# A recurrent attention layer with a Fourier mixer on one core: 64-token steps in quarters of the array, and mixing products of two chunks summed in PSUM

## The chip, the cores and the metric

One core of a Trainium2 chip runs the whole kernel. The metric is the device time of one execution in microseconds (us); the median of three runs of the kernel before is 349.94 us.

## What is computed

The first half is an mLSTM layer, with 4 batch entries, 8 heads, 768 tokens and a head width of 40. For every head a 40x40 state and a normalizer are carried from token to token:

```python
m_new = np.maximum(f_gate[:, :, t] + m, i_gate[:, :, t])
f_stab = np.exp(f_gate[:, :, t] + m - m_new)
i_stab = np.exp(i_gate[:, :, t] - m_new)
C = f_stab * C + i_stab * outer(vt, kt)
n = f_stab * n + i_stab * kt
y[:, :, t] = sigmoid(o_gate) * (C @ qt) / np.maximum(np.abs(n . qt), 1.0)
```

The second half takes x, the heads side by side (4 x 768 x 320), and mixes tokens and channels:

```python
theta = x @ w_theta
zr, zi = x * np.cos(theta), x * np.sin(theta)
u = x + einsum('ts,bsd->btd', w_tok_r, zr) + einsum('ts,bsd->btd', w_tok_i, zi)
out = u + np.maximum(u @ w_ch, 0.0)
```

The four weight matrices arrive in float64 and are handed over as pairs of 32-bit words.

## The kernel before, in words

The 768 tokens are cut into 6 chunks of 128. A unit n is one chunk of one batch entry (24 units, `attention(n)`, L403); a mixer step q is one chunk of a pair of batch entries (12 steps, `mixer(q)`, L534).

**Attention, in chunked form.** A unit makes a 128x128 matrix of decay factors per head in a tile E of 8 x 128 columns. In the first chunk they come out of matmuls (`assemble`, L292) and one exponential per half (L421). In the five others a DMA spreads a row of gate sums over all partitions (L425, from DRAM scratch g_d) and ScalarE takes eight exponentials with a bias per token (L430). GpSimd then zeroes what lies above the diagonal (L436). The scores (`score`, L440) are eight float32 matmuls that contract 64 rows, four in each half of the array's rows. VectorE multiplies scores and factors (L449). The output (`pv`, L457) adds, in one PSUM bank, three matmuls of the scaled queries (`qs`, L453; their factors eb are also spread by a DMA) with the carried state C (L461), and eight full-array matmuls of weights with values (L464; L469 in the first chunk). VectorE makes the denominator (L474, L475), the gate (L480) and x (L486). The state is carried over a chunk by `fade` (L500 or L498), three matmuls (L506), `wane` (L516, L154, L156) and `grow` (L527).

A float32 matmul shows in the trace as two passes, each a weight load (PEld) and a matmul (PE); a float32r matmul shows as one. So the counts of the float32 lines are twice the matmuls of the code.

**Mixer.** x is turned (L542), split in a high and a low part in float32r (L544, L545), added to the accumulator acc (L550), multiplied by w_theta (L557, L563), reduced to a turn (L569, L573), put through sine and cosine (L582, L583), multiplied by x (L588) and split again (L589, L590). Then each of five column groups j takes 12 matmuls of 384 columns (`group`, L596, the line L601) into a two-bank PSUM tile, and VectorE adds that tile to acc (L616). For the first chunk two copies and one shorter add stand in its place (L608, L611, L612). That is 60 groups, each with an add of its own.

**Weights.** `split` (L330) rebuilds float32 from the float64 words on VectorE and ScalarE in seven steps (L338 or L340, L343, L344, L347, L350, L358, L359); two pieces per chunk, three and more elsewhere.

**The end** (`channel`, L620). Once all chunks are mixed, u is split (L656, L657) and multiplied by w_ch (L671, L681), VectorE adds the result (L691), and DMAs store it.

**PSUM.** Three slots of two banks (`two`) serve scores, first-chunk factors, x transposes, theta and mixing; two slots of one bank (`one`) serve the attention output and the state update.

**Order.** Every step is a task with a letter for its engine (T TensorE, V VectorE, A ScalarE, G GpSimd, D a DMA issued by SyncE). A list written out in the code, `ORDER`, gives number and engine of every task; each engine does its own tasks in that order, and waits are added where a tile is shared.

Of the kernel before, what the change touches and what calls it, by code (L numbers as in the profile page):

```python
# [8 lines left out]
F32 = mybir.dt.float32  # L9
# [13 lines left out]
KD = 3 * D  # L23
TOK = 9 * D + H * E1
# [4 lines left out]
HEAD = [3 * g + j for j in range(3) for g in range(3) if 3 * g + j < H]  # L29
RANK = [HEAD.index(h) for h in range(H)]  # L30
SPREAD = (0,)
# [4 lines left out]
LEAST = 2.0**-15  # L36
WCOLS = 1792

ORDER = """
4V 24T 0D 1D 2V 60V 62V 63V 3A 108D 67A 70D 61G 64V 68V 69G 65A 109V 82D 66V 71A 74D 83A 141D 124D 143T 145A 126T 111V  # L40
144A 84V 112V 148T 113V 72D 110G 131T 142D 125D 127A 114V 128A 75A 209T 147G 85V 116V 115D 129G 86V 73A 119T 208D 130G
132V 87A 146G 133V 150V 149V 76V 121V 88A 134T 77V 120A 151T 210A 78V 291D 89G 211A 192T 93A 135V 122A 152V 190D 79A
155G 136V 207D 153V 138G 101D 194A 213G 80A 193A 123D 293D 212G 214T 197T 195G 137V 102A 216V 154V 156T 157A 94D 158T
117T 196G 294D 139T 81G 215V 191D 199V 159A 118A 198V 217T 160V 295D 140V 95A 90A 161A 274D 103V 200T 92A 91A 218V
272D 162T 301G 297A 163T 104V 96V 105V 221G 296A 219V 276D 201V 202V 106A 275D 164A 204G 292D 220V 298G 360D 203V 165V
306G 299T 280T 300V 222T 356D 224T 278A 337D 277A 166V 273D 59G 282G 279G 362A 225V 223V 361A 226V 97V 167A 281V 302T
98V 227A 583D 168A 169V 402D 205T 228T 229T 364T 172V 341D 270D 170V 107G 357D 345T 303V 358D 99A 206A 230A 173A 171V
174V 271A 363G 231V 232V 283T 100G 365V 284V 285V 308G 187T 188V 304V 409D 233A 305V 289G 359D 234A 422D 418D 403A
287A 189V 178T 286V 235G 180V 410V 416D 307T 437D 343A 179V 184T 411V 366G 340D 186V 185V 238G 342A 412V 236A 309V
175T 367T 424A 239V 177V 338D 373A 344G 339D 176V 413V 346V 263D 368V 288T 414A 420D 310T 181T 311A 290V 369V 182V  # L50
312V 371G 347G 370V 441D 404V 419D 237V 348T 372T 352V 405V 183A 314T 423A 315T 354A 421D 442A 240G 313V 440D 406V
445T 439D 426T 374V 425G 415G 443A 316A 264A 317V 353T 444G 427V 244T 250T 355V 318A 446V 417A 428V 407A 433G 319A
349V 265V 320A 429T 253T 587D 350V 438D 351V 266V 267V 252A 268A 408G 246V 256D 324G 257A 245V 434T 255V 487D 435G
447G 436V 325A 483D 486D 430V 241T 488A 431V 251V 555D 448T 258V 489A 502D 259V 485D 321G 260V 247T 506D 254V 449V
452G 484D 242V 491T 450V 504D 248V 432V 322A 261A 454G 243A 510T 249V 490G 375T 451V 503D 507A 492V 376A 453T 505D
493G 508A 498V 262G 509G 455V 589A 648D 494T 377V 379T 326V 500G 499T 568D 588A 694D 495V 517G 511V 456T 380T 378V
381A 501V 269V 457A 496V 591T 512G 585D 323G 562D 382V 590G 383V 513T 564D 385A 458V 566D 556V 584D 695V 389G 331T
459V 384A 592V 386G 519V 586D 332V 569A 570A 565D 514V 563A 598G 515V 460T 652D 461T 516V 462A 572T 463V 327T 593G
328V 594T 390V 653A 497V 521T 567D 518T 571G 573V 574V 654A 391G 629D 464V 335T 524V 595V 466A 729D 522A 523V 333T
520V 596V 465A 387A 336V 525T 633D 388V 655G 467G 334V 656T 635A 634A 637T 600V 468V 526T 470G 597V 527A 557V 471V  # L60
528V 632D 657V 579A 472V 650D 575T 599T 576V 708D 649D 577V 529A 636G 394T 578V 601V 581G 638V 396T 397V 400T 530A
531A 651D 696V 658V 630D 602T 535G 631D 469G 580T 710D 395V 659T 603A 582V 709A 532V 639V 329T 401V 794D 640T 660V
558V 714D 604V 605V 398T 712D 330V 665A 663V 646V 715A 779D 732D 533V 781A 716A 536V 717G 731D 606T 733D 644G 661V
713D 559V 718T 399V 641V 642V 737T 711D 735A 607T 643V 662V 720G 534G 664T 719V 666V 721T 645T 734A 608A 697V 777D
730D 537G 698V 548D 739V 392T 795D 609V 736G 560A 561G 722V 546T 647V 780A 610A 854D 738V 667T 612A 727A 668A 547V
740T 393V 477T 611A 725A 549V 782G 798D 669V 538T 613V 741V 723V 670V 478V 540T 550V 797D 799A 775D 744G 616G 539V
671T 724V 551V 796D 860D 672T 701D 742V 746V 783T 778D 673A 541V 699V 785G 743V 913D 674V 802T 552V 542T 784V 871D
804G 800A 745T 553A 862A 801G 614A 803V 809A 617V 544T 618V 805T 700G 479T 675A 677A 747V 776D 681G 543V 847D 748T
811G 726T 856D 545V 475T 728V 749V 476V 676A 554G 750V 786T 480V 861A 932D 873D 678V 874D 481T 881G 682A 875D 787V
752T 751V 753T 702A 788V 789V 792G 858D 859D 482V 879T 848A 615G 806V 754A 864T 810T 755V 877A 876A 849V 807V 863G  # L70
865V 808V 683G 872D 878G 621T 756A 866V 880V 679V 619T 703V 813T 812V 758A 790G 814A 857D 620V 622V 680G 882T 931D
# [747 lines left out]
```

## Time and profile before

| | |
|---|---|
| runs | 349.94 us median, 349.14 to 351.73, three runs |
| span of the profiled execution, first to last instruction | 347.3 us |
| median of the runs less that span | 2.6 us |
| TensorE matmuls busy | 309.7 us (89% of the span), 2246 passes |
| VectorE (DVE) busy | 297.2 us (86%) |
| ScalarE (ACT) busy | 187.0 us (54%) |
| GpSimd (POOL) busy | 162.3 us (47%) |
| moved by DMA | 59.66 MB |

The page gives the profiled execution's time as its span; the 2.6 us are taken as what lies around it. A row of a group of instructions has, after the count, the time in which at least one of them ran, the mean length of one in ns, and then the idle time of the engine just before them with what ended it. Matmuls and weight loads overlap their neighbours, so for them the first figure divided by the count is the pace, and the mean length is not. PEld is the row of weight loads. [...]

### The profile page before, as it was taken

What the parts mean: (1) busy time and instruction counts of PE and PEld (TensorE: products, weight loads), DVE (VectorE), ACT (ScalarE), POOL (GpSimd) and SP (SyncE); (2) the same over time, 40 slices, a digit from 0 to 9 for tenths busy, and PEclk for the clock granted to TensorE, in tenths of its full rate; (3) what the DMA queues carried; (4) which work ended last, traced back from release to release, by engine and by line L of the source; (5) the groups of instructions that cost most, each with busy time, mean ns of one, the idle gap of its engine ahead of it and who ended that gap; (6) DMA issues with size and microseconds to landing.
All of it is one profiled execution on the core that took longest, in us unless ns stands there. A gap on an engine that the chain in (4) does not pass through costs nothing.

```text
span 347.3 us, 5976 instructions
## 1 busy us (share of the span) xinstructions
PE 309.7 (89%) x2246; PEld 295.6 (85%) x2246; DVE 297.2 (86%) x468; ACT 187.0 (54%) x375; POOL 162.3 (47%) x122
## 2 busy tenths in 40 slices
PE   1559886997999989898979999889999999999994
PEld 0559876987998979798979999889999999998994
DVE  2999999899999998999999969998999796897231
ACT  2857888937767688757539384649334221140000
POOL 0836675645486864531492258552128432644000
PEclk9969998799899989998999999999999999999999
DMA  4968999718469895096557775355301000001423
GB/s 145 346 215 285 327 366 318 271 32 295 162 205 303 262 295 196 9 286 215 165 178 278 259 262 156 98 144 174 116 3 45 2 0 0 2 0 47 161 113 136
DMA packets 20912, 59.66 MB, mean 172 GB/s; under 512 B 2191, under 2 KB 7700, under 8 KB 20884
## 3 DMA queue, kind: packets, MB, share of 16 engines
q1 hardware_dynamic: 20884, 59.28, 51.3%
q8 instruction: 18, 0.29, 0.3%
q14 instruction: 10, 0.08, 0.1%
HBM read 55.17 MB, written 4.10 MB: 171 GB/s over the span
## 4 chain that ended last, share of the span: by engine, by line
PE 54%; DVE 36%; DMA 4%; issue 3%; POOL 1%; ACT 0%; SPq 0%; DVEq 0%; POOLq 0%; ACTq 0%
PE two L601 28%; PE two L671 7%; PE one L464 5%; PE two L557 3%; DVE E L449 3%; PE two L445 3%; DVE val L347 3%; PE one L461 2%; DVE val L343 2%; DVE sg L480 2%; DMA w<-in_gates 2%; DVE val L344 2%; DVE z L590 2%; DVE C L527 2%; DMA tok<-in_tok 2%
## 5 line engine op out<-in xcount | busy, mean ns | idle before, releaser
L601 PE MATMUL two<-w,z 128*128 128x384 f32 x720 | 139.7, 350 | 8.2 <-DVE r L573 5.3
L601 PEld LDWEIGHTS two<-w,z 128*128 128x128 f32 x720 | 129.6, 196 | 10.9 <-DVE r L573 6.3
L616 DVE TENSOR_TENSOR acc<-two,acc 128x768 f32<-128x768 f32 x50 | 46.7, 949 | 8.7 <-PE two L601 8.5
L430 ACT ACTIVATE E<-E,biasT 128x128 f32<-128x128 f32 x160 | 49.4, 391 | 7.3 <-DMA E<-g_d 7.1
L436 POOL TENSOR_SCALAR_AFFINE_SELECT E<-E 128x1024 f32<-128x1024 f32 (+1 forms) x28 | 33.7, 1211 | 33.5 <-ACT E L430 30.9
L464 PE MATMUL one<-tok,E 128*128 128x41 f32 x320 | 42.7, 272 | 0.5 <-issue 0.4
L464 PEld LDWEIGHTS one<-tok,E 128*128 128x128 f32 x320 | 41.0, 193 | 0.9 <-DVE E L449 0.9
L449 DVE TENSOR_TENSOR E<-two,E 128x1024 f32<-128x1024 f32 (+1 forms) x28 | 29.4, 1060 | 2.0 <-POOL E L436 2.0
L461 PE MATMUL one<-C,q 120*128 120x123 f32 (+1 forms) x120 | 26.3, 301 | 2.9 <-DVE C L527 1.3
L671 PE MATMUL two<-u,w 128*128 128x384 f32 x156 | 28.5, 339 | 0.3 <-DVE acc L616 0.3
L445 PE MATMUL two<-qk 64*128 64x128 f32 x384 | 26.0, 285 | 2.8 <-DVE acc L550 1.5
L445 PEld LDWEIGHTS two<-qk 64*128 64x128 f32 x384 | 24.4, 196 | 4.6 <-DVE acc L616 1.8
L671 PEld LDWEIGHTS two<-u,w 128*128 128x128 f32 x156 | 26.8, 188 | 1.6 <-issue 1.0
L588 POOL TENSOR_TENSOR ab<-ab,X 128x640 f32<-128x640 f32 x10 | 16.3, 1631 | 19.5 <-ACT ab L583 19.5
L359 POOL TENSOR_TENSOR w<-val,w 128x768 fp32r<-128x768 f32 x9 | 18.4, 2043 | 13.8 <-ACT w L358 8.6
L691 DVE SCALAR_TENSOR_TENSOR acc<-two,acc 128x768 f32<-128x768 f32 x10 | 9.3, 954 | 17.2 <-PE two L681 9.3
L557 PE MATMUL two<-wth,xs 128*128 128x320 f32 x144 | 23.5, 312 | 0.5 <-DVE acc L550 0.5
L453 POOL TENSOR_TENSOR q<-q,eb 120x384 f32<-120x384 f32 x12 | 14.6, 1219 | 16.6 <-PE two L445 11.4
L557 PEld LDWEIGHTS two<-wth,xs 128*128 128x128 f32 x144 | 21.5, 188 | 0.9 <-issue 0.9
L461 PEld LDWEIGHTS one<-C,q 120*128 120x128 f32 x120 | 18.9, 192 | 4.0 <-issue 2.5
L590 POOL TENSOR_TENSOR z<-r,z 128x640 fp32r<-128x640 f32 x9 | 16.0, 1778 | 10.4 <-ACT z L589 5.3
L569 ACT ACTIVATE r<-two 128x640 f32<-128x640 f32 x11 | 7.7, 701 | 23.8 <-PE two L563 23.5
(120 smaller groups left out, 540.3 us busy)
## 6 DMA issues: line engine op xcount, KB each, us to landing
qk<-in_qk SPq DMA_DIRECT2D x24, 512.0 KB, 5.7
E<-g_d SPq DMA_DIRECT2D x20, 512.0 KB, 4.6
raw<-in_wtok SPq DMA_DIRECT2D x12, 768.0 KB, 7.0
tok<-in_tok SPq DMA_DIRECT2D x24, 344.0 KB, 6.5
out<-acc SPq DMA_DIRECT2D x10, 384.0 KB, 2.5
q<-in_q SPq DMA_DIRECT2D x20, 180.0 KB, 4.6
eb<-e_d SPq DMA_DIRECT2D x20, 180.0 KB
sg<-in_og SPq DMA_DIRECT2D x5, 640.0 KB, 7.7
```

The lines of the kernel that those rows point to most:

```text
L359: add(name + "_lo", "GV", lambda e: ENG[e].tensor_sub(lo(), v(), hi().bitcast(F32)), [val, *rest], step)
L430: nc.scalar.activation(u.E.t[:, r], u.E.t[:, r], AF.Exp, bias=biasT[:, c, b * H + r:b * H + r + 1])
L436: nc.gpsimd.affine_select(d, d, pattern=[[0, k], [1, P]], compare_op=ALU.is_ge, fill=0.0, base=0, channel_multiplier=-1)
L445: nc.tensor.matmul(u.sc.t[:, f, hp], u.qk.t[rows, 1, hp], u.qk.t[rows, 0, hp], start=True, stop=True)
L449: add(f"wg{n}{a}", "V", lambda e, a=a, z=z: nc.vector.tensor_mul(u.E.t.rearrange("p (f k) t -> p f (k t)", f=2)[:, a:z], u.sc.t[:, a:z], u ...
L461: nc.tensor.matmul(u.ph.t[:, 3 * g * E1:h1 * E1], u.q3.t[:KD, g, :], C[b][:, 3 * g:h1, :].rearrange("p h e -> p (h e)"), start=True, stop= ...
L464: nc.tensor.matmul(u.ph.t[:, h * E1:(h + 1) * E1], u.E.t[:, RANK[h], :], u.tok.t[:, 9 * D + h * E1:9 * D + (h + 1) * E1], start=False, sto ...
L557: nc.tensor.matmul(th.t[:, b, :DM], xs.t[:, x, k], wt5[:, y, k], start=(i == l == 0), stop=False)
L590: add(f"zl{q}{s}", "GV", lambda e, s=s, src=src: ENG[e].tensor_sub(zv(1, s), src.t, zv(0, s).bitcast(F32)), [src, z], n + 1.5)
L601: nc.tensor.matmul(pm.t[:, t, :TH], z.t[:, x, s, j * P:(j + 1) * P], wv(c, y, s, t), start=(k == 0), stop=(k == 5))
L616: add(f"ga{q}{j}", "V", lambda e, j=j, pm=pm, av=av: nc.vector.tensor_add(av, pm.t[:, :, :TH], av), [pm], n + 2.6 + 0.3 * j, swap="acc")
L671: nc.tensor.matmul(pm[jj].t[:, t, :TH], wcv(x)[:, col:col + P], up[pr, k][:, y, ts], start=(i == l == 0), stop=(jj == 2 and i == 4 and l = ...
```

## The change

Attention works in steps of 64 tokens: a unit is still 128 tokens of one batch entry, but it holds two steps. Its decay factors are 8 x 64 columns instead of 8 x 128, one step in one half of the partitions. All four products of a unit (scores, state update, carried state times query, weights times values) are 64-row, 64-column float32 matmuls that address the four quarters of the array in turn. The decay factors come from four float32r matmuls in every chunk, with the mask inside, so the DMAs that spread gate rows, the eight exponentials per unit and GpSimd's select are gone, and with them q3, eb, g_d and e_d. The state is kept in two copies per batch entry and carried twice per unit. The carried part leaves PSUM scaled by `pa` and is added by `hv`.

PSUM becomes four slots of two banks, for everything.

The mixing products of two consecutive chunks are added up in one PSUM tile before VectorE adds it to acc; `GROUPS` says which chunks go together, for each pair of batch entries.

`split` loses its clamp (a scaled absolute value on ScalarE takes its place) and its absolute value is always on ScalarE. Some steps may run on other engines, sigmoid works in halves, and `ORDER` is new.

The core of the diff, without the new order, the gate preparation (`gate_part`, which writes every gate sequence twice, shifted by 64 tokens) and the data layout:

```diff
+L = P // 2
+GROUPS = [[(0,), (1, 2), (3, 4), (5,)], [(0, 1), (2, 3), (4,), (5,)]]
...
-    two = slots("two", 3, [2, 512], pool=ps)
-    one = slots("one", 2, [512], pool=ps)
+    two = slots("two", 4, [2, 512], pool=ps)
...
-    E_k = slots("E", 3, [H, P], pool=ap)
+    E_k = slots("E", 3, [2, 4 * L], pool=ap)
...
-            nc.vector.tensor_scalar_max(v(), v(), LEAST)
-            nc.vector.tensor_scalar(vi(), vi(), 3, 0x3FFFFFF8, op0=ALU.logical_shift_left, op1=ALU.bitwise_and)
+        add(name + "_abs", "A", lambda e: nc.scalar.activation(v(), words(1).bitcast(F32), AF.Abs, scale=LESS), [rawt, val], step)
+        add(name + "_up", "V", lambda e: nc.vector.tensor_scalar(vi(), vi(), 3, None, op0=ALU.logical_shift_left), [val], step)
...
     def attention(n):
+        u.dd, u.sc, u.it, u.ph = Tile(two), Tile(two), Tile(two), Tile(two)
+        def assemble(e):
+            o = lambda f: u.dd.t[:, f, :4 * L].rearrange("p (k t) -> p k t", t=L)
+            for f in range(2):
+                nc.tensor.matmul(o(f), W(c)[:, f], M[:, b], start=True, stop=False)
+            for f in range(2):
+                nc.tensor.matmul(o(f), place[:, 2 * b + f], Gm(c), start=False, stop=True)
+        add(f"exp{n}", "A", lambda e: nc.scalar.activation(u.E.t, u.dd.t[:, :, :4 * L], AF.Exp), [u.dd, u.E], n - 0.5, table="exp")
+        def score(e):
+            for k in range(4):
+                for f in range(2):
+                    for x in range(2):
+                        s = slice(L * x, L * x + L)
+                        nc.tensor.matmul(u.sc.t[half[x ^ f], f, k * L:(k + 1) * L], q4(1)[half[f], k, s],
+                                         q4(0)[half[f], k, s], start=True, stop=True)
+        add(f"wg{n}", "V", lambda e: nc.vector.tensor_mul(u.E.t, u.sc.t[:, :, :4 * L], u.E.t), [u.sc, u.E], n)
+        def state(e):
+            for k in range(4):
+                for f in range(2):
+                    for x in range(2):
+                        r = half[x ^ f]
+                        h = 4 * f + k
+                        nc.tensor.matmul(u.st.t[half[f], x, k * E1:(k + 1) * E1], u.tok.t[r, h * D:h * D + L],
+                                         vt()[r, h], start=True, stop=True)
+        def carry(x):
+            add(f"cw{x}{n}", "GV", lambda e: ENG[e].tensor_mul(C[b][1 - x], C[b][x], f), (), n + 0.2)
+            add(f"up{x}{n}", "V", lambda e: nc.vector.tensor_add(C[b][1 - x], sv(x), C[b][1 - x]), [u.st], n + 0.3)
+        def inter(e):
+...
+                        nc.tensor.matmul(u.it.t[half[x], f, k * E1:(k + 1) * E1], q4(0)[half[f], k, s], C[b][x][half[f], k],
+                                         start=True, stop=True)
+        def intra(e):
+...
+                        nc.tensor.matmul(u.ph.t[half[x], f, k * E1:(k + 1) * E1], u.E.t[r, f, k * L:(k + 1) * L],
+                                         vt()[r, 4 * f + k], start=True, stop=True)
+        add(f"pa{n}", "VA", passed, [u.it, u.hv], n + 0.4)
+        add(f"hv{n}", "V", lambda e: nc.vector.tensor_add(hv4(), v4(u.ph), hv4()), [u.ph, u.hv], n + 0.5)
...
     def mixer(q):
+        mine = next(g for g in GROUPS[pr] if c in g)
+        if c != mine[-1]:
+            return
-                            nc.tensor.matmul(pm.t[:, t, :TH], z.t[:, x, s, j * P:(j + 1) * P], wv(c, y, s, t),
-                                             start=(k == 0), stop=(k == 5))
+                            nc.tensor.matmul(pm.t[:, t, :TH], Z[cc, pr].t[:, x, s, j * P:(j + 1) * P], wv(cc, y, s, t),
+                                             start=(k == 0 and cc == mine[0]), stop=(k == 5 and cc == mine[-1]))
+            for cc in mine:
+                add(f"mix{cc * 2 + pr}{j}", "T", lambda e, cc=cc, group=group: group(e, cc), [Z[cc, pr], w[cc], pm], n + 2.5 + 0.3 * j)
```

Read from the two order lists: the passes of the mixing (720) and of theta, the transposes and the end stay as they are. VectorE's adds of mixing tiles go from 60 to 40. Of the tasks that may run on either of two engines, `zm` goes from 7 to 17 on VectorE, `zl` from 9 to 12, `zh` from 12 to 6, the mixer's `abs` from 6 to 3, `xhi` from 3 to 1, `gb` from 7 to 2, x (`X`) from 24 to 14. TensorE passes between whole-array tasks and tasks in halves or quarters of the array 74 times, against 38. In TensorE's part of the new list, the first products of three column groups (steps 1 of the mixer) stand next to each other, ahead of the second products of step 3, so that three of the four PSUM slots are held between them.

## Rows read from the trace of the kernel before

**Rows 1.** Three stages: busy us of each engine, PEclk, DMA share, GB/s
```profile
0.00:170.00 170.00, 141.83 (x1084) 133.78 (x1085) 157.35 (x268) 119.66 (x240) 90.66 (x77) 0.93 0.72 237
170.00:315.00 145.00, 140.25 (x996) 136.15 (x994) 128.18 (x188) 67.36 (x135) 70.21 (x46) 1.00 0.33 107
315.00:347.30 32.30, 27.63 (x172) 25.70 (x168) 11.63 (x13) 0.00 (x0) 1.46 (x1) 1.00 0.32 123
sum 347.30, PE 309.71 PEld 295.63 DVE 297.16 ACT 187.02 POOL 162.34; mean PE 103.24 PEld 98.54 DVE 99.05 ACT 62.34 POOL 54.11
```

**Rows 2.** The chain that ended last, by engine, whole span
```profile
PE 54%; DVE 36%; DMA 4%; issue 3%; POOL 1%; ACT 0%; SPq 0%; DVEq 0%; POOLq 0%; ACTq 0%
```

**Rows 3.** Timeline, TensorE's first attention matmuls: start us, us
```profile
12.46 0.79 PE L298 MATMUL two<-selr,z 64*128 64x512 f32 x2 [9.90 <-DVE z L285]
```

**Rows 4.** Groups by line and form, weight loads of TensorE
```profile
L464 PEld LDWEIGHTS one<-tok,E 128*128 128x128 f32 x320 | 41.0, 193 | 0.9 <-DVE E L449 0.9
L461 PEld LDWEIGHTS one<-C,q 120*128 120x128 f32 x120 | 18.9, 192 | 4.0 <-issue 2.5 <-DVE q L453 1.3
L506 PEld LDWEIGHTS one<-tok 128*120 128x120 f32 x120 | 15.1, 189 | 3.5 <-issue 2.0 <-DVE C L527 0.8 <-DVE X L486 0.2
L469 PEld LDWEIGHTS one<-tok,E 128*128 128x128 f32 x64 | 8.9, 226 | 0.0
L445 PEld LDWEIGHTS two<-qk 64*128 64x128 f32 x384 | 24.4, 196 | 4.6 <-DVE acc L616 1.8 <-DVE acc L550 1.7 <-issue 0.4
L601 PEld LDWEIGHTS two<-w,z 128*128 128x128 f32 x720 | 129.6, 196 | 10.9 <-DVE r L573 6.3 <-DVE E L449 1.8 <-DVE acc L616 1.1
L557 PEld LDWEIGHTS two<-wth,xs 128*128 128x128 f32 x144 | 21.5, 188 | 0.9 <-issue 0.9
```

**Rows 5.** Timeline of TensorE in the end stage: start us, us
```profile
325.12 1.31 PE L681 MATMUL two<-u,w 64*128 64x384 f32 x12
326.36 9.63 PE L671 MATMUL two<-u,w 128*128 128x384 f32 x54
```

**Rows 6.** Groups by line and form, VectorE
```profile
L616 DVE TENSOR_TENSOR acc<-two,acc 128x768 f32<-128x768 f32 x50 | 46.7, 949 | 8.7 <-PE two L601 8.5
L612 DVE COPY acc<-two 128x384 f32<-128x384 f32 x7 | 3.8, 542 | 0.0
L343 DVE TENSOR_SCALAR val<-val 128x768 f32<-128x768 f32 x12 | 9.5, 791 | 0.0
L340 DVE TENSOR_SCALAR val<-raw 128x768 int32<-128x768 int32 x4 | 3.7, 939 | 0.0
L449 DVE TENSOR_TENSOR E<-two,E 128x1024 f32<-128x1024 f32 x20 | 24.2, 1212 | 1.9 <-POOL E L436 1.8
L449 DVE TENSOR_TENSOR E<-two,E 128x512 f32<-128x512 f32 x8 | 5.1, 680 | 0.2 <-POOL E L436 0.2
L486 DVE TENSOR_TENSOR X<-one,sg 128x320 f32<-128x320 f32 x24 | 11.3, 482 | 0.4
L453 DVE TENSOR_TENSOR q<-q,eb 120x384 f32<-120x384 f32 x8 | 6.2, 774 | 0.0
L527 DVE SCALAR_TENSOR_TENSOR C<-one,tab,C 120x123 f32<-120x123 f32 x32 | 9.3, 332 | 3.3 <-PE one L506 3.3
L588 DVE TENSOR_TENSOR r<-r,X 128x640 f32<-128x640 f32 x5 | 4.1, 812 | 0.0
L590 DVE TENSOR_TENSOR z<-ab,z 128x640 fp32r<-128x640 f32 x6 | 6.9, 1154 | 0.0
L589 DVE CAST z<-ab 128x640 fp32r<-128x640 f32 x7 | 3.9, 556 | 0.0
```

**Rows 7.** Groups by line and form, ScalarE and GpSimd
```profile
L430 ACT ACTIVATE E<-E,biasT 128x128 f32<-128x128 f32 x160 | 49.4, 391 | 7.3 <-DMA E<-g_d 7.1
L436 POOL TENSOR_SCALAR_AFFINE_SELECT E<-E 128x1024 f32<-128x1024 f32 x20 | 26.9, 1347 | 30.9 <-ACT E L430 30.9
```

**Rows 8.** The page's list of DMA issues: count, KB each, us to landing
```profile
E<-g_d SPq DMA_DIRECT2D x20, 512.0 KB, 4.6
```

More of the change, by code (lines that the diff above doesn't have):

```diff
@@ L43 @@
[L43 to L47, printed above, removed]
@@ L330, in split, with masks, places @@
-    def split(name, hi, lo, raw, n, uses, step, scale=None):
+    for b in range(B):
+        add(f"clear_c{b}", "GV", lambda e, b=b: ENG[e].memset(C[b][0], 0.0), (), -8.0 + b)
+    def masks(b):
+        add(f"mask{b}", "GV", lambda e: ENG[e].tensor_tensor(
+            M[:, b], T["sel"][:, 4 * b:4 * b + 4].unsqueeze(2).broadcast_to([P, 4, L]),
+            T["tri"].unsqueeze(1).broadcast_to([P, 4, L]), op=ALU.add), (), -9.0 + b)
+    def places(b):
+        add(f"place{b}", "GAV", lambda e: COPY[e](
+            place[:, 2 * b:2 * b + 2].rearrange("p f (g t) -> p (f g) t", t=L),
+            T["place"][:, 4 * b:4 * b + 4].unsqueeze(2).broadcast_to([P, 4, L])), (), -9.0 + b)
@@ L361, in raw_load @@
+        add(name + "_lo", "GV", lambda e: ENG[e].tensor_sub(lo(), o(), hi().bitcast(F32)), [val, *rest], step)
     def raw_load(name, src, step):
         t = Tile(raw_k)
-        load(name + "_ld", lambda: dma(t.t[:, :src.shape[-1]], src), [t], step - 2)
-        return t
+        n = src.shape[-1]
+        load(name + "_ld", lambda: dma(t.t[:, :n], src), [t], step - 2)
+        return t, lambda k: t.t[:, :n].bitcast(I32).rearrange("p (n k) -> p n k", k=2)[:, :, k]
+    same = lambda v: v
     def theta_weights():
@@ L433, in attention @@
[L433 to L438 removed]
+        q4 = lambda x: u.qk.t[:, x].rearrange("p (k t) -> p k t", t=P)
+        kt = lambda: u.tok.t[:, :H * D].rearrange("p (h d) -> p h d", d=D)
@@ L501, in attention @@
-        add(f"fade{n}", "GVA", fade, [u.tok], n + 0.4)
+            ENG[e].tensor_mul(kt(), kt(), f.unsqueeze(2).broadcast_to([P, H, D]))
+        add(f"fade{n}", "GVA", fade, [u.tok], n + 0.1)
+        u.st = Tile(two)
         def state(e):
-            for g in range(3):
-                n1 = min(3, H - 3 * g) * E1
-                nc.tensor.matmul(u.st.t[:KD, 3 * g * E1:3 * g * E1 + n1], u.tok.t[:, g * KD:(g + 1) * KD],
-                                 u.tok.t[:, 9 * D + 3 * g * E1:9 * D + 3 * g * E1 + n1], start=True, stop=True)
@@ L529, in attention @@
-        add(f"up{n}", "AV" if c == 0 else "V", grow, [u.st], n + 0.6)
-    done = {}
+            for k in range(4):
[5 more added lines that the diff above has]
+                                         vt()[r, h], start=True, stop=True)
+        add(f"st{n}", "T", state, [u.tok, u.st], n + 0.2, half=True)
@@ new lines, in attention @@
+        add(f"it{n}", "T", inter, [u.qk, u.it], n + 0.3, half=True)
+        def intra(e):
+            for k in range(4):
+                for f in range(2):
+                    for x in range(2):
+                        r = half[x ^ f]
+                        nc.tensor.matmul(u.ph.t[half[x], f, k * E1:(k + 1) * E1], u.E.t[r, f, k * L:(k + 1) * L],
+                                         vt()[r, 4 * f + k], start=True, stop=True)
+        add(f"ph{n}", "T", intra, [u.E, u.tok, u.ph], n + 0.3, half=True)
@@ L735, in mlstm_mixer @@
             mixer(n // 2)
[L736 removed]
+    names = {f"X{n}" for n in range(NU - 4, NU)}
     channel()
```

615 lines of the change are left out of this document (273 added, 342 removed).

## The prediction

> **What bounds the kernel now.** I read the busy time by stage first. In the first 170 us VectorE is the engine that is full: 157.4 of 170 us, with TensorE at 141.8 and at a granted clock of 0.93. From 170 to 315 us it is TensorE, 140.3 of 145 us at full clock. From 315 us to the end TensorE runs the last products almost alone [rows 1]. The chain of waits says the same in one line: 54% of the span on TensorE, 36% on VectorE [rows 2]. So neither engine can be relieved alone: a faster attention on TensorE helps the second stage, fewer adds on VectorE the first, and since the mixing products can be done early or late, work can be shifted between the two. TensorE's first attention matmul starts at 12.46 us [rows 3]. Up to 315 us it is busy for 141.8 + 140.3 = 282.1 us, so it stands still for 315 - 12.5 - 282.1 = 20.4 us after its start. I use that figure below as "stalls".
>
> **TensorE, what goes.** The weight loads give its pace. Attention's four products with whole-array passes keep it for 41.0 us (320 passes), 18.9, 15.1 and 8.9 us, and the scores for 24.4 us: 108.3 us [rows 4]. Per pass that is 41.0/320 = 128 ns in the whole array, with only 41 columns moving, and 15.1/120 = 126 ns with up to 123: the load of 128 weight columns sets the pace, not what streams. A score pass, with half the rows, takes 24.4/384 = 64 ns, so a pass in the upper half and one in the lower half run in the 128 ns of one. All of these include some low clock and the tails of each group.
>
> **TensorE, what comes.** 24 units x 4 products x 16 matmuls x 2 passes = 3072 passes, in rounds of four that address four different quarters: 768 rounds. A quarter loads 64 weight columns, half of 128. No row shows two column halves at work side by side, so I bound a round from both sides. If all four quarters overlap as the two row halves do, a round takes half of 128 ns, 64 ns, 49 us in all; it can't be less, since the pace above goes with the weight columns. If the two column halves of the same rows take turns, it is 128 ns, 98 us. If nothing overlaps, 256 ns, 197 us. I take 80 ns, 61.4 us: nearest to the score row, where sharing the array is free, and a quarter more for eight instructions that must be dealt out in that time. The new factors are 24 x 4 = 96 float32r passes of 256 columns; 384 columns take 129.6/720 = 180 ns and 320 take 21.5/144 = 149 ns, so 256 take about 118 ns: 11.3 us. (The gate transposes, and the first chunk's old factors, are left out on both sides.) Changing between whole and divided array costs too: twelve half-array passes at the end take 326.36 - 325.12 = 1.24 us, where six pairs at 9.63/54 = 178 ns would take 1.07; that is 0.17 us for a change in and one out [rows 5]. 74 - 38 = 36 more changes at 0.085 are 3.1 us; 0.25 each would be 9. In all 75.8 us for 108.3: 32 us less; from 45 less to 4 more with the two inner bounds, 103 more with the outer one.
>
> **VectorE.** Mixing: 20 adds fewer at 0.949 us are 19.0; five pairs of copies fewer, 0.54 for the longer and by its rate 0.36 for the shorter, are 4.5; five own adds twice as long give back 0.7. That is 23 less. Weights: twelve clamps at 0.791 (9.5), with the shorter ones by their columns about 12.5 in all, and 3.7 for absolute values that move to ScalarE; three more casts at 0.6 come: 14 less. The shift alone I leave at its present cost. Attention: the weighting takes 24 x 0.68 = 16.3 us instead of 24.2 + 5.1; ten x fewer, 4.8; qs 6.2 gone; pa (19) and hv (24) are PSUM reads of 328 columns, as x is with 320 at 0.482: 20.7 more; 44 state updates of 164 columns, by 0.332 for 123 about 0.37, are 16, in place of 18 tasks of three pieces each, which comes to as much; 16 cw at 0.35 are 5.6, of which I count 3, as the old scaling of the state goes. All that is about 1 less; if pa and hv cost as much as a weighting of 512 columns, 0.68, it is 7 more. Mixer: ten more zm at 0.81 and three more zl at 1.15 against eleven fewer casts and absolute values at about 0.65: 4 more [rows 6]. Sum: 23 + 14 + 1 - 4 = 34 us less, 263 in place of 297.
>
> **ScalarE, GpSimd, DMA.** 160 exponentials, 49.4 us, become 24 larger ones; what is put on ScalarE instead (seven more fades of eight pieces, five pa, more casts) I put at no more than that, so it stays near 190 us and bounds nothing. GpSimd loses the select, 26.9 us and more, and with it the step that VectorE waited behind [rows 7]. The spread of gate rows, 20 DMAs of 512 KB [rows 8], and its two companions go; the DMA share of the first stage is 0.72 [rows 1], so this may shorten waits there and I count nothing for it.
>
> **Waits.** A mixing tile of two chunks stays in its PSUM slot until the second chunk's products are in. Behind a matmul that waits for a slot stands everything else on TensorE, and behind that VectorE's next adds. I count nothing, and carry it as a rival.
>
> **The sum.** Up to the end stage TensorE needs 12.5 us until it starts, 282.1 - 32.5 = 249.6 us of work and 20.4 us of stalls: 282.5. VectorE, with 157.4 + 128.2 - 34 = 251.6 us and the 29.4 us that it has free now, comes to 281. The two stay level. The end stage is not touched: 32.3 us. That makes a span of 314.8 us and, with the 2.6 us by which the median of the runs stands above the profiled span, 317.4. I say 318 us, 9% less than 349.94.
>
> **Rivals.**
> *A. Column halves take turns.* TensorE then works 4 us more than before, while VectorE has 34 us less: 12.5 + 286 + 32.3 + 2.6 = 333 us and stalls. With all 20.4 us of these it is 353; with half of them, as VectorE is no longer full, 343. I say 344. For it: no row shows two column halves at once. Against it: in the whole array loads and matmuls of the same rows do run side by side, with pace 128 ns for a load that is listed at 193 ns [rows 4]. [...]
> *B. Slower: four PSUM slots.* Factors, scores, both outputs, state update, transposes, theta and mixing all use the same four slots: 24 x 5 + 24 + 40 + 2 = 186 uses by the end stage, after 283 us. Four slots give 4 x 283 = 1132 us, 6.1 us for each use. From a mean hold of 6.1 us on the slots decide; at 7 us it is 186 x 7 / 4 = 326 us, and 326 + 32.3 + 2.6 = 361 us. For it: 20 tiles hold two chunks' products. Against it: one chunk's twelve matmuls take 12 x 0.18 = 2.2 us and the add 0.95, and most other tiles are read within a step or two.
> *C. Slower: nothing overlaps.* 103 us more on TensorE, about 453 us. Only if quarters behave unlike row halves.
> *D. Faster still.* Rounds at 64 ns (12 us less) and half of the stalls gone with the DMA rows, the select and VectorE's waits (10 us): 296 us.
>
> **How the numbers follow.** My forecast has 0.55, A 0.18, B 0.11, C 0.03, D 0.13. About 1% is what a measurement of this kernel can tell from no change, so faster means under 346.4. The forecast and D are faster, A in half of its cases (0.09), which gives 0.77; same has 0.08, the rest of A mostly; slower 0.15, B, C and the top of A. The range goes from 294, just under D, to 354, past A with all its stalls, and leaves out B, C and the far side of D; the forecast's own range is 306 to 332.
>
> **What would show it.** Right: a task of 32 quarter passes lasts about 0.6 us (20 ns a pass); VectorE near 263 us in all with 40 adds of mixing tiles; weight loads in total near 263 us; the end stage still about 32 us. A: such a task lasts 1.0 us, and TensorE is over 95% busy up to the end stage. B: gaps on TensorE that end with a VectorE instruction which reads PSUM, all over the middle. The forecast fails if a quarter pass takes 32 ns or more, or if both engines show long gaps at once.

## The result and the profile after

The changed kernel takes 328.62 us (median of four runs, 328.12 to 330.03) against 349.54 us for the kernel before in the same set of runs. The ratio is 0.940, with a 95% interval of 0.9345 to 0.945: 21 us faster, where 32 were forecast. The profiled execution spans 326.8 us.

The page of the changed kernel: its span, the busy time of each engine, the granted TensorE clock (PEclk) in 40 slices, in tenths of full speed, the DMA queue of kind "instruction" (packets, MB, share), and the chain that ended last.

```profile
span 326.8 us, 10220 instructions
...
PE 286.1 (88%) x4436; PEld 264.8 (81%) x4436; DVE 253.9 (78%) x449; ACT 178.2 (55%) x358; POOL 106.6 (33%) x103
...
PEclk9767857999999999999999999999999999999999
...
q8 instruction: 35, 0.57, 0.7%
...
PE 59%; DVE 22%; ACT 9%; issue 5%; DMA 3%; SPq 1%; POOL 1%; DVEq 1%; POOLq 0%; ACTq 0%
```

VectorE has gone from 297.2 to 253.9 us and from 36% of the chain [rows 2] to 22%. TensorE's pass count has doubled (2246 to 4436), yet its weight loads are down from 295.6 [rows 1] to 264.8 us. The stages, from TensorE's first attention matmul at 11.33 us on, with the columns of [rows 1]:

```profile
11.33:60.00 48.67, 36.07 (x681) 33.31 (x682) 37.33 (x75) 37.68 (x79) 14.33 (x17) 0.72 0.61 213
60.00:170.00 110.00, 98.54 (x1930) 90.52 (x1928) 93.93 (x177) 69.58 (x148) 44.29 (x42) 1.00 0.47 158
170.00:294.80 124.80, 118.73 (x1633) 113.41 (x1633) 103.88 (x167) 65.29 (x120) 41.91 (x33) 1.00 0.19 63
294.80:327.00 32.20, 26.54 (x171) 24.92 (x169) 12.65 (x12) 0.00 (x0) 5.14 (x3) 0.98 0.31 123
```

The end stage starts at 294.8 instead of 315 us and still takes 32 us (to the span's end at 326.8). Before it no engine is full any more: between 60 and 170 us TensorE has 98.5 of 110 us and VectorE 93.9. TensorE stands still for 12.6, 11.5 and 6.1 us in the three stages, 30.1 us in all.

Groups of the changed kernel that answer to [rows 4] and [rows 6]. L573 is the mixing (L601 before), L423, L444, L460 and L469 are scores, state update, carried state and weights times values in quarters, L411 and L413 the new factors; L341, L342, L344 are the three integer steps of a weight piece, L490 the gate, L426 the weighting, L481 and L483 `pa` and `hv`, L486 the absolute value of the denominator, L596 the add of mixing tiles.

```profile
L573 PEld LDWEIGHTS two<-w,z 128*128 128x128 f32 x720 | 125.3, 189 | 2.6 <-DVE z L559 1.1 <-DVE C L452 0.7 <-issue 0.4
...
L460 PEld LDWEIGHTS two<-C,qk 64*64 64x64 f32 x768 | 15.5, 142 | 6.7 <-issue 2.3 <-ACT acc L517 1.7 <-ACT E L415 1.6
L469 PEld LDWEIGHTS two<-tok,E 64*64 64x64 f32 x768 | 15.4, 142 | 4.9 <-issue 3.1 <-DVE hv L481 1.0 <-ACT E L415 0.2
L444 PEld LDWEIGHTS two<-tok 64*64 64x64 f32 x768 | 15.1, 147 | 5.5 <-issue 3.9 <-POOL tok L434 0.8 <-ACT val L156 0.2
L423 PEld LDWEIGHTS two<-qk 64*64 64x64 f32 x768 | 15.1, 149 | 7.4 <-ACT val L156 6.1 <-issue 0.8 <-DVE r L542 0.2
...
L411 PEld LDWEIGHTS two<-M,wg 128*128 128x128 f32 x48 | 8.5, 210 | 6.2 <-ACT wg L156 3.2 <-DVE hv L481 1.4 <-DVE acc L596 0.8
L413 PEld LDWEIGHTS two<-wg,placer 128*128 128x128 f32 x48 | 8.5, 217 | 0.0
...
L596 DVE TENSOR_TENSOR acc<-two,acc 128x768 f32<-128x768 f32 x30 | 28.4, 951 | 10.6 <-PE two L573 10.5
L426 DVE TENSOR_TENSOR E<-two,E 128x512 f32<-128x512 f32 x24 | 16.3, 683 | 4.6 <-PE two L423 4.4
L490 DVE SCALAR_TENSOR_TENSOR sg<-den,sg 128x320 f32<-128x320 f32 x24 | 14.1, 597 | 0.3
L344 DVE SCALAR_TENSOR_TENSOR val<-raw,val 128x768 int32<-128x768 int32 x12 | 12.3, 1029 | 0.1
L342 DVE SCALAR_TENSOR_TENSOR val<-raw,val 128x768 int32<-128x768 int32 x12 | 12.2, 1020 | 0.1
L486 DVE TENSOR_SCALAR den<-hv 128x8 int32<-128x8 int32 x24 | 10.4, 434 | 0.3
L483 DVE TENSOR_TENSOR hv<-two,hv 128x328 f32<-128x328 f32 x24 | 11.9, 494 | 5.2 <-PE two L469 3.7 <-ACT hv L479 1.3
L481 DVE TENSOR_TENSOR hv<-two,leaveT 128x328 f32<-128x328 f32 x19 | 9.3, 492 | 3.7 <-PE two L460 3.5
L341 DVE TENSOR_SCALAR val<-val 128x768 int32<-128x768 int32 x12 | 6.6, 551 | 0.0
```

The four quarter products load weights for 61.1 us, 19.9 ns a pass and 79.6 ns a round of four. The waits of TensorE's matmuls (waited for: us, times, longest) show what stands behind the idle time:

```profile
PE two L423 <- ACT val L156: 6.0, 1, 6.0
PE two L510 <- DVE X L493: 3.9, 4, 1.4
PE two L329 <- DVE w L308: 3.0, 1, 3.0
PE two L411 <- ACT wg L156: 2.9, 2, 2.2
PE two L444 <- issue: 2.3, 2, 1.5
PE two L469 <- issue: 2.2, 3, 1.0
PE two L460 <- ACT acc L517: 1.6, 1, 1.6
...
PE two L460 <- issue: 1.4, 2, 1.0
...
PE two L573 <- DVE z L559: 0.8, 1, 0.8
...
PE two L329 <- issue: 0.3, 1, 0.3
```

Two things are new. The four "issue" rows, 6.2 us in all, are waits for nothing that the profile shows; the kernel before had 0.4 us of them. And the first scores wait 6.0 us, until 21.18. The row names a ScalarE step that ended at 21.10, but the scores need nothing of it; what they need is the third of the queries' DMAs, which was issued at 13.33 us, behind the second gate load, and landed at 21.04. The mixing itself (L573) hardly waits any more: 2.6 us of idle time ahead of its weight loads, where L601 had 10.9 [rows 4].

### The profile page after: what moved, and what is told of

Its sections match the earlier page's. It is cut to its first block, busy times and chain, and to the rows that moved or that the text cites. A ratio compares the mean times of both kernels' runs of the same rounds, so it can differ in the third digit from the quotient of the medians.

```text
span 326.8 us, 10220 instructions
## 1 busy us (share of the span) xinstructions
PE 286.1 (88%) x4436; PEld 264.8 (81%) x4436; DVE 253.9 (78%) x449; ACT 178.2 (55%) x358; POOL 106.6 (33%) x103
## 4 chain that ended last, share of the span: by engine, by line
PE 59%; DVE 22%; ACT 9%; issue 5%; DMA 3%; SPq 1%; POOL 1%; DVEq 1%; POOLq 0%; ACTq 0%
PE two L573 27%; PE two L650 8%; PE two L526 4%; PE two L444 3%; PE two L423 3%; PE two L460 3%; DVE sg L490 2%; PE two L510 2%; DVE den L486 2%; PE two L469 2%; DVE hv L483 2%; DVE ab L557 2%; DMA raw<-in_wth 2%; DVE X L493 2%; PE two L532 2%
## 5 line engine op out<-in xcount | busy, mean ns | idle before, releaser
L573 PE MATMUL two<-w,z 128*128 128x384 f32 x720 | 133.3, 341 | 1.2 <-DVE z L559 0.8
L573 PEld LDWEIGHTS two<-w,z 128*128 128x128 f32 x720 | 125.3, 189 | 2.6 <-DVE z L559 1.1
L596 DVE TENSOR_TENSOR acc<-two,acc 128x768 f32<-128x768 f32 x30 | 28.4, 951 | 10.6 <-PE two L573 10.5
L451 POOL TENSOR_TENSOR C<-C,wane 128x164 f32<-128x164 f32 x28 | 16.4, 590 | 42.2 <-PE two L460 34.0
L350 POOL TENSOR_TENSOR w<-val,w 128x768 fp32r<-128x768 f32 (+1 forms) x11 | 19.4, 1766 | 32.1 <-DVE w L349 18.7
L423 PE MATMUL two<-qk 64*64 64x64 f32 x768 | 17.6, 238 | 6.0 <-ACT val L156 6.0
L460 PE MATMUL two<-C,qk 64*64 64x41 f32 x768 | 18.2, 235 | 4.6 <-ACT acc L517 1.6
L423 PEld LDWEIGHTS two<-qk 64*64 64x64 f32 x768 | 15.1, 149 | 7.4 <-ACT val L156 6.1
L460 PEld LDWEIGHTS two<-C,qk 64*64 64x64 f32 x768 | 15.5, 142 | 6.7 <-issue 2.3
L469 PE MATMUL two<-tok,E 64*64 64x41 f32 x768 | 18.1, 235 | 3.2 <-issue 2.2
L432 ACT ACTIVATE tok<-tok,fadeT 128x40 f32<-128x40 f32 x88 | 20.4, 316 | 0.4 <-DMA tok<-in_tok 0.4
L444 PE MATMUL two<-tok 64*64 64x41 f32 x768 | 17.6, 239 | 2.9 <-issue 2.3
L426 DVE TENSOR_TENSOR E<-two,E 128x512 f32<-128x512 f32 x24 | 16.3, 683 | 4.6 <-PE two L423 4.4
L444 PEld LDWEIGHTS two<-tok 64*64 64x64 f32 x768 | 15.1, 147 | 5.5 <-issue 3.9
L469 PEld LDWEIGHTS two<-tok,E 64*64 64x64 f32 x768 | 15.4, 142 | 4.9 <-issue 3.1
L340 ACT ACTIVATE val<-raw 128x768 f32<-128x768 f32 (+3 forms) x16 | 13.4, 842 | 10.8 <-DMA raw<-in_wtok 8.6
```

The lines of the kernel that those rows point to most:

```text
L350: add(name + "_lo", "GV", lambda e: ENG[e].tensor_sub(lo(), o(), hi().bitcast(F32)), [val, *rest], step)
L423: nc.tensor.matmul(u.sc.t[half[x ^ f], f, k * L:(k + 1) * L], q4(1)[half[f], k, s], q4(0)[half[f], k, s], start=True, stop=True)
L426: add(f"wg{n}", "V", lambda e: nc.vector.tensor_mul(u.E.t, u.sc.t[:, :, :4 * L], u.E.t), [u.sc, u.E], n)
L432: nc.scalar.mul(kt()[:, h], kt()[:, h], f[:, h:h + 1])
L444: nc.tensor.matmul(u.st.t[half[f], x, k * E1:(k + 1) * E1], u.tok.t[r, h * D:h * D + L], vt()[r, h], start=True, stop=True)
L451: add(f"cw{x}{n}", "GV", lambda e: ENG[e].tensor_mul(C[b][1 - x], C[b][x], f), (), n + 0.2)
```

## The experiments

Times are medians in us; each has its own runs of the kernel before beside it. The changed kernel itself came out at 328.62 and, in a later set, at 329.83, so differences of one or two us between kernels of different sets mean nothing.

### How quarters overlap: three other orders of the same matmuls

The 16 matmuls of each quarter product are issued in another order, by the row half r, column half c and head k that they address.

```diff
+KEY = lambda r, c, k: (r, c, k)   # e1_same: four in a row in one quarter
+KEY = lambda r, c, k: (r, k, c)   # e2_cols: column halves of the same rows alternate
+KEY = lambda r, c, k: (c, k, r)   # e3_rows: row halves of the same columns alternate
...
-            for k in range(4):
-                for f in range(2):
-                    for x in range(2):
+            for k, f, x in turns_of(lambda f, x: (f, x ^ f)):
```

> All sixteen matmuls of a product sorted by quarter: four in a row use the same quarter of the array. Theory (quarters overlap because different quarters are addressed in turn, about 20 ns a pass, 80 ns a round): a pass now takes about the load of 64 weight columns, 50 to 60 ns, so the 3072 quarter passes take some 160 us of weight loads instead of 61, and the time rises to 400 to 430 us. Rival (the 20 ns are the pace at which instructions are dealt out, whatever quarter they address): 61 us as before and no change in time.

> Neighbours address the two column halves of the same 64 rows, first all of the upper rows and then all of the lower ones. Theory (column halves overlap like row halves): two passes in 55 to 64 ns, about 30 ns a pass, 95 us of quarter passes and 345 to 365 us in all. Rival (a weight load overlaps only with passes in other rows): 50 to 60 ns a pass, the same as with one quarter in a row, 400 to 430 us.

> Neighbours address the two row halves of the same 64 columns. Both theories expect overlap of two: about 30 ns a pass, 95 us of quarter passes, 345 to 365 us. If it is clearly faster than the run with column halves, rows overlap better than columns.

Measured: 380.69 (ratio 1.0955, 1.0795 to 1.1115), 337.09 (0.970, 0.952 to 0.988) and 331.88 (0.955, 0.941 to 0.969), two runs each, and all three less than was expected. The weights-times-values loads (L469, in the three kernels L465) over a stretch at full clock, 170 to 290 us: PE busy (count), PEld busy (count), clock, DMA share, GB/s. First the changed kernel, then the three in the order above.

```profile
170.00:290.00 120.00, 5.25 (x256) 4.58 (x256) 1.00 0.19 66
```

```profile
170.00:290.00 120.00, 13.97 (x320) 12.90 (x320) 1.00 0.32 108
```

```profile
170.00:290.00 120.00, 8.79 (x320) 7.78 (x320) 1.00 0.24 80
```

```profile
170.00:290.00 120.00, 7.11 (x262) 6.21 (x257) 1.00 0.21 69
```

PEld busy over count: 17.9 ns a pass in four quarters, 40.3 in the same quarter, 24.3 with two column halves, 24.2 with two row halves. So column halves share the array as well as row halves do here, and four quarters do better than two halves. These figures hold the tail of every task. From the start of one weight load to the start of the next within a task, the same stretch gives 13.7, 38, 22 and 22 ns. That settles rival A: if column halves took turns, e2_cols would have the pace of e1_same; the traces have 24.3 against 40.3 ns.

The loads of e1_same come to 145.8 us in place of 61.1, 84.7 more, and the time grew by 52. Part of the 84.7 goes with a lower clock: 0.50 from 11.33 to 60 us, where the changed kernel has 0.72. From 170 to 290 us, at full clock, the loads of the four products take 41.4 ns in e1_same and 17.9 in the changed kernel; at that pace 3072 would come to 127.3 and 55.1 us, 18.5 and 6.0 less than measured, so some 12 of the 84.7 lie outside the full-clock pace, as an estimate. Even this kernel, with TensorE 95% busy, pays only 0.6 us per us of loads: its matmuls are busy for 73.4 us more, and TensorE's idle time falls from 40.7 to 19.5 us. The other two pay less still: e2_cols has 23.5 us more loads than the changed kernel and takes 8.5 us longer, e3_rows 22.7 more for 3.3, which is 0.36 and 0.14 per us (0.45 and 0.24 if the ratios to the kernel before are compared).

### What the sums over two chunks are worth

e4_single takes 15 of the 20 sums apart again; the first chunk's add stands right behind its products.

```diff
-GROUPS = [[(0,), (1, 2), (3, 4), (5,)], [(0, 1), (2, 3), (4,), (5,)]]
+GROUPS = [[(0,), (1,), (2,), (3,), (4,), (5,)], [(0, 1), (2,), (3,), (4,), (5,)]]
```

> 15 of the 20 sums of two chunks in PSUM are taken back: each of these column groups of one chunk is added to acc by itself, right behind its products; all else, order included, stays. VectorE gets 15 adds of 0.95 us more, 14.3 us. Theory (VectorE and TensorE level): 4 to 10 us slower. Rival 1 (VectorE has 73 us free, adds are hidden): within 1.5 us. Rival 2 (slots held for two chunks cost more than the adds save): faster by 2 us or more.

Measured: 354.01 (1.020, 1.008 to 1.031), 25 us slower, which none of the theories had. To see whether the place of the new adds made it, e7_single_late has the same `GROUPS`, but each of these adds comes up to four VectorE tasks later.

> 15 sums of two chunks taken back as before, but the add of the first chunk stands up to four VectorE tasks behind its products (always ahead of the second chunk's products) and not right behind them. Theory (half of the 25 us came from VectorE standing still behind an add that waits for TensorE): 337 to 346 us. Rival (the 25 us are the price of 15 more uses of the PSUM slots, wherever the adds stand): 350 us or more.

Measured: 346.36 (0.990, 0.986 to 0.995). So 8 of the 25 us were the place, and 18 remain. To price VectorE's time alone, e6_pad keeps the sums and gives VectorE 15 more instructions of the size of an add, behind the adds, without a PSUM tile of their own.

```diff
                     nc.vector.tensor_add(av, pm.t[:, :, :TH], av)
+                    if len(mine) > 1:
+                        nc.vector.tensor_max(av, av, av)
```

> Each of the 15 adds of a two-chunk sum to acc is followed by one more VectorE operation over the same 768 columns (the maximum of acc with itself, which changes nothing), 14 to 15 us in all. No PSUM slot is held longer, TensorE does nothing more. If VectorE's time is what the sums save, this is slower by 5 to 14 us; if what the run without sums lost (25 us) came from waits for slots and from the place of its adds, this is under 4 us slower.

Measured: 337.53 (0.961, 0.949 to 0.974), 8.9 us slower. Its padding group:

```profile
L599 DVE TENSOR_TENSOR acc<-acc 128x768 f32<-128x768 f32 x15 | 16.4, 1095 | 0.5
```

VectorE got 14.2 us more to do here and 10.3 in e7_single_late (268.1 and 264.2 against 253.9), yet the latter costs twice as much. The waits of e7_single_late (L574 mixing, L597 its add) show the rest:

```profile
DVE acc L597 <- PE two L574: 14.2, 12, 2.4
PEld two L574 <- DVE acc L597: 10.1, 9, 2.5
PE two L574 <- DVE acc L597: 9.2, 9, 2.2
```

Mixing products wait 9.2 us for a slot that an add must free, and adds 14.2 us for products. In the changed kernel TensorE has no such wait for an add at L573, and VectorE's wait is 10.5. So about half of what the sums give is VectorE's time; the other half fits these waits, which come with 15 more fills and releases of PSUM slots.

### The weights without their clamp

e5_clamp puts the clamp and the masked shift back on VectorE.

```diff
-        add(name + "_up", "V", lambda e: nc.vector.tensor_scalar(vi(), vi(), 3, None, op0=ALU.logical_shift_left), [val], step)
...
+            nc.vector.tensor_scalar_max(v(), v(), LEAST)
+            nc.vector.tensor_scalar(vi(), vi(), 3, 0x3FFFFFF8, op0=ALU.logical_shift_left, op1=ALU.bitwise_and)
...
```

The unscaled absolute value and the sign mask that belong to the clamp go back with it.

> The weight rebuilding gets its clamp and its two-step shift back (absolute value stays on ScalarE); all else stays. VectorE gets one operation more in each of 15 pieces and a longer shift, some 14 us, most of it in the first 170 us. Theory (VectorE's work counts about half, as both engines are level): 5 to 9 us slower. Rival (TensorE and waits set the time, VectorE has 73 us free): within 2 us.

Measured: 335.44 (0.960, 0.952 to 0.9675): 6.8 us for 9.9 us of VectorE, where some 14 were expected. The two steps in its trace:

```profile
L344 DVE TENSOR_SCALAR val<-val 128x768 int32<-128x768 int32 x12 | 8.0, 664 | 0.4
L343 DVE TENSOR_SCALAR val<-val 128x768 f32<-128x768 f32 x12 | 7.0, 585 | 0.0
```

The same clamp took 791 ns in the kernel before [rows 6] and the same masked shift 1005. So what shortened the shift to 551 ns was mostly not its simpler form. Sorting the records of the kernel before by what ran beside them points to the cause. Of its twelve masked shifts of 768 columns, the four with no GpSimd instruction beside them take 559 to 561 ns; the five slow ones, 1144 to 2194 ns, all have one over more than three quarters of their length. The other three take 560 or 561 ns too, one of them with GpSimd beside it for 0.92 of its length, so not every neighbour costs time. Of its 24 gates, twelve have none beside them and take 439 to 493 ns; the twelve others take 626 to 1519, and the nine slowest of these, 967 and more, have one over three quarters of their length or more. In e5_clamp eleven of the twelve masked shifts have none beside them and take 559 to 561 ns, the twelfth 1805. No run took GpSimd's work away and left all else, so the link rests on this sorting.

### The two new stalls

e8_early issues the first queries and tokens ahead of the second gate load. In SyncE's part of the order, by name:

```diff
-gates1 tok1 tok2 qk0 qk1 qk2
+qk2 qk0 qk1 tok1 tok2 gates1
```

> The loads of the first three units (qk 0 to 2, tok 1 and 2) are issued ahead of the second gate load, at which SyncE stands for some 6 us until the gate tile is free. TensorE waits 6 us for the first of them at 21 us. Theory (the start is set by this queue): 3 to 6 us faster. Rival (what is gained at the start is lost to later waits, the gates arriving later): within 1 us.

Measured: 330.62 (0.945, 0.936 to 0.953): no gain. Its trace has the first scores without a wait (timeline: start, us) and, a little later, a new one (waits; L461 is the carried state there):

```profile
14.02 2.04 PE L424 MATMUL two<-qk 64*64 64x64 f32 x96
```

```profile
PE two L461 <- DVE E L427: 9.0, 1, 9.0
```

The scores start 7 us earlier, and 9 us of waiting turn up behind them. The 6 us alone were not the bound of the first stage. e10_hot asks the same of its low clock, with 17 pairs of the warming matmuls (`heat` in the code; nothing uses what they compute) among the first attention products (12 behind st0, 5 behind sc4 in the order).

> 17 pairs of warming matmuls are added on TensorE: 12 behind the first state product, where it waits 6 us for a load, and 5 ahead of the first mixing products. They fill idle time and compute nothing that is used. The granted clock is 0.72 from 11 to 60 us. Theory (the low clock in the first 60 us is paid for): the clock rises above 0.85 there and the time falls by 2 to 5 us. Rival (loads, ScalarE and VectorE set the first 60 us): the clock rises and the time stays within 1.5 us or grows.

Measured: 329.48 (0.9395, 0.932 to 0.947), as without them, although the clock of the first stage went from 0.72 to 0.87:

```profile
11.33:60.00 48.67, 42.20 (x810) 34.16 (x812) 40.04 (x80) 40.09 (x84) 14.22 (x17) 0.87 0.60 213
```

One execution each suggests that the clock paid at first. The matmul with 3600 more to come starts at 60.8 us in this trace and at 63.2 in the changed kernel's, the one with 2500 to come at 118.7 and 121.4. With 2000 to come the lead is gone: 162.1 and 162.0. On the way the granted clock is 0.94 from 60 to 90 us and 0.91 from 120 to 140, where the changed kernel has 1.00, and the "issue" stalls, which come next, are 9.3 us in place of 6.2. So the run shows no gain in time, but not that the clock costs nothing.

The other new stall is "issue". The changed kernel's timeline of TensorE at its first place, between two quarter products of one task:

```profile
24.89 0.75 PE L444 MATMUL two<-tok 64*64 64x41 f32 x22
27.12 0.37 PE L444 MATMUL two<-tok 64*64 64x41 f32 x10 [1.48 <-issue]
```

I counted where in TensorE's list of instructions (two for each pass) such a gap stands, over 450 ns and with no semaphore on the next instruction. In the changed kernel: 450, 706, 1729, 2242, 2498, 3778, 7362, 8130. Each is 193 or 194 above a multiple of 256. e9_shift makes the list 128 instructions longer near its start: the first warming tasks are cut into smaller matmuls.

```diff
-            for i in range(8):
-                nc.tensor.matmul(t.t[:, i % 2], ones[:, :P], ones, start=True, stop=True)
+            for i in range(40):
+                nc.tensor.matmul(t.t[:, i % 2, :96], ones[:, :P], ones[:, :96], start=True, stop=True)
```

> The two warming tasks at the start become 40 short matmuls each in place of 8 long ones, so that TensorE's list is 128 instructions longer ahead of the first real matmul; nothing else changes. In the changed kernel TensorE stands still inside quarter products, waiting for nothing that the profile shows, 6.2 us in all, and the eight longest of these gaps come at instructions 450, 706, 1729, 2242, 2498, 3778, 7362 and 8130 of its list, which differ by multiples of 256. Theory (instructions are brought in blocks of 256 and the quarter products use them up faster than the next block comes): the gaps stay at the same places of a block, so they move 128 instructions forward in the work, to other products; their sum may change. Rival (something in these products holds them): the gaps stay at the same products, 128 instructions later in the list. Either way the time moves by no more than 5 us.

Measured: 325.72 (0.928, 0.920 to 0.936). Its gaps stand at 706, 2242, 2498, 4033, 6082, 7361, 7618: again 193 or 194 above a multiple of 256, now at other products:

```profile
25.56 0.74 PE L460 MATMUL two<-C,qk 64*64 64x41 f32 x22
26.85 0.37 PE L460 MATMUL two<-C,qk 64*64 64x41 f32 x10 [0.55 <-issue]
```

So it is the place in the list that stops TensorE, not what stands there. The "issue" waits still come to 6.2 us. To see whether the 3 us of gain are real, both kernels ran again in one set, six runs each.

> The kernel with TensorE's list 128 instructions longer, once more and beside the changed kernel on the same chip, in five rounds. Theory (what it gains is the place of the block boundaries and a higher clock up to 60 us): 2 to 5 us under the changed kernel. Rival (the 3 us seen are the spread of the runs): within 1 us of it.

> The changed kernel itself, in the same five rounds, for the comparison with the one before it: 328 to 330 us.

Measured: 328.26 (0.939, 0.9346 to 0.9435) for the shifted list and 329.83 (0.947, 0.944 to 0.9505) for the changed kernel. The ratios differ by 0.8%, and their intervals just miss each other; the single runs overlap (324.89 to 330.66 and 328.62 to 331.48). A gain of 2 to 3 us is likely, but not safe. Nor would it be the list's alone: the clock from 11.33 to 60 us is 0.81 in the one and 0.69 in the other. In these two runs 14 of 16 gaps stand at such places; the other two, of 661 ns, are at theta's half-array products.

## Why the prediction came out as it did

The direction and the mechanism were right, and the time lies in the range; it is 10.6 us above the point, inside the forecast's own range of 306 to 332. Step by step:

- **Quarters, right, in part by luck.** 80 ns a round were taken, 79.6 came. At full clock, from 170 to 290 us, it is 71.6; from 11.33 to 60 us, at a clock of 0.72, a pass takes 27.4 ns, 110 a round, which the 80 did not provide for. Start to start, a round takes 55 ns, below the 64 of which I said "it can't be less". The 128 ns that the 64 are half of are no floor: from 170 to 290 us, at full clock, the whole-array loads of the kernel before (L464) start 112 ns apart in the median, and their busy time over count, 127 ns, holds the tails and pauses of every task. A task of 32 passes took 0.68 us at full clock where about 0.6 was to show.
- **Weight loads in all, right by two errors that cancel.** 263 us forecast, 264.8 measured. The new factors take 17.0 us for 96 passes instead of 11.3; the mixing, held constant, went from 129.6 to 125.3. Of the changes between whole and divided array I counted 74, but that takes in those between halves and quarters; between whole and divided there are 63, which makes the term 2.1 us in place of 3.1.
- **VectorE, 9 us too high.** 263 forecast, 253.9 measured. `pa` and `hv` were right (21.2 against 20.7), the weighting too (16.3). What failed is "the shift alone I leave at its present cost": it fell from 12.1 to 6.6 us, the other two integer steps and the gate by 9.1 more (14.2, 14.7 and 18.8 us before). I had taken the durations of before as a property of the instruction, while by the sorting above part of them was GpSimd running beside it. That GpSimd would lose the select I had counted for the wait behind it alone. These 14.6 us are more than the 9 because other terms came out higher. The largest is the absolute value of the denominator, which I held constant: L486 takes 10.4 us, and 3.6 before.

```profile
L474 DVE TENSOR_SCALAR den<-one 128x8 int32<-128x8 int32 x24 | 3.6, 150 | 0.0
```

- **End stage, right.** 32.3 us forecast, 32.0 measured.
- **The sum, its term "20.4 us of stalls" failed.** Forecast up to the end stage: 12.5 + 249.6 + 20.4 = 282.5. Measured: 11.3 + 253.3 + 30.1 = 294.7. Of the 9.7 us more of stalls, 1 us was there before: so much of TensorE's 282.1 us lies ahead of 12.46 us, so the stalls of before were 21.5, and the work as much less. Another 7.8 are the "issue" gaps and the wait of 1.6 us put down to L517, which belongs to them (see the last section); the trace of before has 0.4 us of "issue" waits on TensorE. What is left is under 1: without these gaps the three stages have 10.8, 7.4 and 4.1 us of stalls, against 8.8, 7.9 and 4.8 before. What bounds the first stage is open.
- **Why stalls cannot be kept constant.** I said the two engines "stay level", each as full as before. They are not: VectorE stands free for 72.9 of 326.8 us instead of 50.1. With both engines well below full, a us more on either cost less than a us: 0.6 on TensorE in e1_same (52 for 84.7), but 0.36 and 0.14 in e2_cols and e3_rows; 0.6 to 0.7 on VectorE (6.8 for 9.9 in e5_clamp, 8.9 for 14.2 in e6_pad). So a saving of 32 us on both should not have been taken in full.
- **Rival A fell** by e2_cols. **Rival B had the wrong sign:** I feared that tiles of two chunks hold PSUM slots longer; without the sums the time is 18 us longer, half of it more than VectorE's time accounts for. **C** fell with A; e1_same, where no two neighbours use different quarters except at the ends of a row of four, gives its price as 381 us and not 453. **D**: the rounds came near its pace at full clock, but its smaller stalls did not come.

Taken alone, the sums (18 us) and the clamp (7 us) exceed the 21 us of the whole change, so the parts do not add up. With 15 of the sums undone and the rest of the change in place (e7_single_late) only 1% is left. What attention in quarters gives alone, in an order of its own, was not run, nor what the new order and the steps moved between engines give.

## What to carry to other kernels

Where two engines are each about 80% busy and wait for each other in turn, don't count a microsecond on either in full, and don't carry the old stalls over as a constant. Here it was worth between a seventh and two thirds, by where it fell. Fewer PSUM tiles with more products in each can be worth twice the instructions that they save: 18 us here, where 15 instructions of that size cost 8.9. Before taking an instruction's duration from a trace, sort its records by what ran beside it: behind the mean of 1005 ns stood 560 alone and, in five of the six records with GpSimd over most of them, 1144 to 2194. And doubling the number of instructions can bring a stall that the old trace hardly had: 6.2 us of "issue" here, 0.4 before.

## What the runs showed of the hardware beyond the forecast

In these products column halves of the divided array overlap as row halves do: 24.3 ns a pass at full clock in e2_cols and 24.2 in e3_rows. Four quarters in turn reach 17.9 in the changed kernel, against 40.3 with four passes in a row in one quarter in e1_same.

TensorE's gaps, as counted above, lie 193 or 194 instructions above a multiple of 256 in its list, all but the two at theta's half-array products, and the list has as many such places as the page has packets of kind "instruction". The page of the kernel before lists the "instruction" queue with 18 packets:

```profile
q8 instruction: 18, 0.29, 0.3%
```

The changed kernel's has 35, of 16 KB each. TensorE's records (loads, matmuls and some 70 semaphore steps) are 4559 and 8949. The places 194, 450, 706 and so on up to the end of a list of that length number 18 and 35, one for each packet; e9_shift, with 9077 records, has 35 of either.

The times of the single packets in the traces tie them to the gaps. In the changed kernel a packet is under way from 24.76 to 25.82 us, and L444 goes on at 27.12. All eight gaps end so, 1.30 to 1.52 us after a packet has landed. The wait of 1.6 us that the table of waits puts down to ScalarE (L517) is a ninth: it stands at 2754, again 194 above a multiple of 256, and ends at 90.22 us, 1.38 after a packet's landing, while the ScalarE step had ended at 89.60. If the n-th packet is taken to bring the block behind the place after the n-th, TensorE passes no place in any trace sooner than 1.05 us after its packet has landed; in the changed kernel the soonest is 1.24.

My reading of these rows, an inference and not a measurement, is a list that comes in blocks of 256 instructions, one with each packet, which short passes use up faster than they arrive. A block is 128 passes: as an estimate from the paces above, 1.8 us of quarters in turn at 13.7 ns, and 4.9 us at 38 ns. A packet takes 0.88 to 1.76 us in the changed kernel, and its block is in use 1.3 us later at the soonest in the gaps. In e1_same, with the same list at 40 ns a pass, no quarter product has such a gap, and TensorE reaches every place at least 2.0 us after its packet has landed; in the kernel before it is 12 us. No run took the transfers away, so the link is one of time and place in every trace, not an experiment.
